# Squares of o summed in pairs of rows before the product with ones

## The chip, the cores and the metric

The kernel runs on one core of a Trainium2 chip. Its time is the device time of one execution in microseconds; three runs gave 1356.24, 1356.35 and 1356.97, a median of 1356.35. The engines are called PE (matrix products; PEld its weight loads), ACT, DVE, POOL and SP, as in the profile.

## The reference, cut to what matters

```python
kv = einsum('bhsd,bhse->bhde', k, v)            # 8 batches, 8 heads, 576 tokens, 64 wide
out = einsum('bhsd,bhde->bhse', q, kv)
rms = sqrt(mean(out * out, axis=-1) + 1e-06)    # over the 64 of one head
x = (out / rms * g_norm), heads side by side    # 4608 tokens x 512
h = x @ w_in;  g = softplus(h);  y = g @ w_out  # 512 -> 2048 -> 512
m = max(y @ w1, y @ w2, y @ w3)                 # 512 -> 768
return m @ w_out2                               # 768 -> 512
```

All is float32.

## The kernel before, in words

Tokens run along the free dimension. The 4608 tokens are done in five passes of twice 456 or 464 tokens (`NS`); in a pass every large layer is a set of products over 2x2 blocks. Pass 0 multiplies the blocks plainly and meanwhile converts the weights and stores their sums; passes 1 to 4 use seven products for eight (`run_group`, `ORDER`), with the sums of weight blocks loaded again. Each float32 operand is split into a high part that PE reads in its faster format (`F32R`) and a low part, the rest, so that one product is three instructions on PE (`mm3`, lines 155 to 157): high by high, high by low, low by high. ACT makes the high part (`cast`, L139), DVE or POOL the low part by a subtraction (`split`, L145).

Attention works on pairs of heads, so that a pair's 2 x 64 values of d fill 128 rows. For each batch `kv_mm` takes k as the stationary operand and v as the moving one and makes, for each of four pairs, two 64x64 blocks on the diagonal of a 128x128 matrix that is zero elsewhere (`heads_mm`, L513); `kv_evict` splits it into `kvh` and `kvl`. `out_mm` multiplies it with q (tokens along the free dimension): o, 128 rows (a pair's two heads, one above the other) by 456 or 464 tokens, in a bank of PSUM. The square chain then follows, 8 times a pass:

- `square`: ACT squares o into `sq` (L635), ACT casts it to `sh` (L139), DVE or POOL subtracts to `sl` (L145), ACT scales o by the gain into `og` (L638).
- `ssq_mm`: two products with `ones` (L645 with sh, L646 with sl), added in one bank, `ss`. `ones` is 1 in two 64x64 blocks on the diagonal, so that every row of ss holds the sum of squares of its head.
- `root` (L175) and `norm` (L653 to L661): reciprocal root, refined once, times og: x.

The first pass makes its o in the opening with unsplit operands (`square32`, `ssq_mm32`, `ones32`); this has no low part. For passes 1 to 4 the eight chains are made beside the products of the pass before, in its last layers but one (`attention_beside`), 32 chains in all. `at(t + 0.4, square, ...)` and `at(t + 4.8, ssq_mm, ...)` give each step its place in an order that is written in units of six PE instructions; `t` grows by 6 from chain to chain.

Events are traced in the order of these times, and a planner then orders each engine's instructions by its own estimate of when their inputs are ready. Where `pinned` is used, an engine's instructions keep the traced order from event to event: all engines in the opening, SP and ACT in the end of pass 0 (the first of the four stretches with chains), SP alone around the starts of passes and through pass 1, and elsewhere none. The chain's tiles come from one set of ten (`ctile`), and o and ss from two banks (`at`; ss of the first stretch has bank `W`).

The host lays out the inputs before the launch (`_laid_out`): `vp` is v by pairs of heads, `gn` the gain for 128 rows, `w_in` with its rows in the order of x.

Of the kernel before, what the change touches and what calls it, by code (L numbers as in the profile page):

```python
# [8 lines left out]
F32 = mybir.dt.float32  # L9
F32R = mybir.dt.float32r  # L10
I32 = mybir.dt.int32
U32 = mybir.dt.uint32
AF = mybir.ActivationFunctionType
ALU = mybir.AluOpType

B, H, S, D = 8, 8, 576, 64
NT, DM, DFF, DF2 = B * S, H * D, 2048, 768
P = 128
NS = (456, 464, 464, 464, 456)
NPASS = len(NS)  # L20
TOK = [2 * sum(NS[:i]) for i in range(NPASS + 1)]
NMAX = max(NS)
NP = H // 2
NC = 5
REST = 64
SHARED = 2
KC = DM // P
# [40 lines left out]
def kernel(  # L68
# [12 lines left out]
    nc = tc.nc  # L81
# [23 lines left out]
    def psum(tag, name):  # L105
        return ps.tile([P, 512], F32, tag=tag, bufs=PS_BUFS[tag], name=name)

    def wide(pool, tag, bufs, name, n, dtype=F32):
        return pool.tile([P, NMAX], dtype, tag=tag, bufs=bufs, name=name)[:, 0:n]

    def ctile(name, n, dtype=F32):
        return wide(cp, "c", 10, name, n, dtype)
# [7 lines left out]
    def xr_tile(p, name, n):  # L120
        return xc_tile(name, n) if p == 0 else wide(rp, "xr", 8, name, n)
# [7 lines left out]
    ones = const.tile([P, P], F32R, name="ones")  # L129
    ones32 = const.tile([P, P], F32, name="ones32")  # L130
    kvs = []
    for s in range(2):
        hi = const.tile([P, NP, P], F32R, name=f"kvh{s}")
        lo = const.tile([P, NP, P], F32R, name=f"kvl{s}")
        kvs.append((hi, lo))

    def cast(eng, hi, src):
        if eng is nc.scalar:
            nc.scalar.copy(hi, src)  # L139
        else:  # L140
            eng.tensor_copy(hi, src)

    def split(eng_hi, src, hi, lo, eng_lo):
        cast(eng_hi, hi, src)
        eng_lo.tensor_tensor(out=lo, in0=src, in1=hi.bitcast(F32), op=ALU.subtract)  # L145
# [4 lines left out]
    def sub(eng, o, a, b):  # L150
        eng.tensor_tensor(out=o, in0=a, in1=b, op=ALU.subtract)  # L151
# [315 lines left out]
    kv_t, q_t, kv_ps = {}, {}, {}  # L467
    qs, o_t, sq_t, ss_t, og_t, ra_t = {}, {}, {}, {}, {}, {}
# [29 lines left out]
    def chunks(b, p):  # L498
        def at_(parts, c):
            return next(t[:, c - cs.start] for t, cs in parts if c < cs.stop)  # L500

        whole = NC - (b < SHARED)
        for c in range(whole):
            yield [at_(parts, c) for parts in kv_t[b, p]]
        if b < SHARED:
            rows = slice(p % 2 * REST, (p % 2 + 1) * REST)
            yield [at_(parts, NC - 1)[rows] for parts in kv_t[b, p - p % 2]]

    def heads_mm(acc, b, p):
        for c, (k, v) in enumerate(chunks(b, p)):  # L510
            for j in range(2):
                r = slice(j * D, (j + 1) * D)
                nc.tensor.matmul(acc[r, r], k[:, r], v[:, r], start=(c == 0), stop=(c == NC - 1))  # L513

    def kv_mm(b):
        kv_ps[b] = psum("at", "kvps")
        for p in range(NP):
            heads_mm(kv_ps[b][:, p * P:(p + 1) * P], b, p)

    def kv_evict(b):  # L520
        hi, lo = kvs[b % 2]
        src = kv_ps.pop(b).rearrange("r (p d) -> r p d", p=NP)
        blocks = [(slice(j * D, (j + 1) * D), slice(None), slice(j * D, (j + 1) * D)) for j in range(2)]
        for b in blocks:
            cast(nc.scalar, hi[b], src[b])
        for b in blocks:
            sub(nc.vector, lo[b], src[b], hi[b].bitcast(F32))


    kv32 = {}  # L530
# [6 lines left out]
    def kv_mm32(b, p):  # L537
        acc = kv_ps[b, p] = psum("at", "kvps")[:, 0:P]
        if b + p:
            heads_mm(acc, b, p)  # L540
            return
        for c, (k, v) in enumerate(chunks(b, p)):
            nc.tensor.matmul(acc, k, v, start=(c == 0), stop=(c == NC - 1))
        warm(2)
# [9 lines left out]
    def kv_evict32(b, p, eng):  # L554
        src, dst = kv_ps.pop((b, p)), kv32[b, p]
        for j in range(2):
            r = slice(j * D, (j + 1) * D)
            cast(eng, dst[r, r], src[r, r])

    def kv_split(b):  # L560
        hi, lo = kvs[b % 2]
# [68 lines left out]

    def square(a, n, p):
        o = o_t.pop((a, p))
        sq = ctile("sq", n)
        sh, sl = ctile("sh", n, F32R), ctile("sl", n, F32R)
        nc.scalar.activation(sq, o, AF.Square)  # L635
        split(nc.scalar, sq, sh, sl, nc.vector if p % 2 or a < TOK[2] or a in TOK else nc.gpsimd)
        og = xr_tile(1, "og", n)
        nc.scalar.mul(og, o, gcol)  # L638
        sq_t[a, p] = (sh, sl)
        og_t[a, p] = og  # L640

    def ssq_mm(a, n, p, tag="at"):
        sh, sl = sq_t.pop((a, p))
        ss = psum(tag, "ss")[:, 0:n]
        nc.tensor.matmul(ss, ones, sh, start=True, stop=False)  # L645
        nc.tensor.matmul(ss, ones, sl, start=False, stop=True)  # L646
        ss_t[a, p] = ss

    def norm(a, n, p):
# [353 lines left out]

    for t in (ones, ones32, *kvs[0], *kvs[1]):
        nc.gpsimd.memset(t if t is ones32 else t.bitcast(F32), 0.0)
    for j in range(2):
        r = slice(j * D, (j + 1) * D)
        nc.gpsimd.memset(ones[r, r].bitcast(F32), 1.0)
        nc.gpsimd.memset(ones32[r, r], 1.0)
    nc.gpsimd.memset(epsc, EPS)  # L1010

    def load_gain():
# [101 lines left out]
    for n, step in enumerate(OPENING):  # L1114
        name, _, opt = step.partition(":")
        kind, *index = name.split(".")
        t = OPEN + 0.25 * n
# [61 lines left out]
def _laid_out(inputs):  # L1179
    import numpy as np  # L1180

    q, k, v = inputs["q"], inputs["k"], inputs["v"]

    def rows(a):

        a = a.reshape(B, NP, 2, S, D).transpose(0, 1, 3, 2, 4).reshape(B, NP, S, P)
        a = np.pad(a, ((0, 0), (0, 0), (0, NC * P - S), (0, 0)))
        a[:SHARED, 0::2, -REST:] = a[:SHARED, 1::2, S - REST:S]
        return np.ascontiguousarray(a.reshape(B, NP, NC, P, P).transpose(0, 1, 3, 2, 4)).reshape(B, NP, P, NC * P)

    def cols(w):

        n = w.shape[1] // P
        return np.ascontiguousarray(w.reshape(KC, P, n, P).transpose(2, 1, 0, 3)).reshape(n, P, KC * P)


    wo = inputs["moe_w_out"].reshape(4, 2, 2, P, 2, 2, P).transpose(0, 5, 4, 3, 2, 1, 6)

    w2 = inputs["moe2_w_out"].reshape(3, 2, P, 2, 2, P).transpose(3, 2, 1, 4, 0, 5)
    w2 = w2.reshape(2, P, 2, 3, 2, P).transpose(3, 0, 1, 2, 4, 5)  # L1200
    w2 = np.ascontiguousarray(w2).reshape(6, P, DM)
    return {
        "qt": np.ascontiguousarray(q.transpose(1, 3, 0, 2)).reshape(NP, P, NT),
        "kp": rows(k),
        "vp": rows(v),
        "gn": np.tile(inputs["g_norm"], 2).reshape(P, 1),
        "w_in": cols(inputs["moe_w_in"]),
        "w_out": np.ascontiguousarray(wo).reshape(NF, P, DM),
        "w123": np.ascontiguousarray(
            np.stack([cols(inputs[f"moe2_w{j}"]) for j in (1, 2, 3)], axis=1)  # L1210
        ),
        "w2_out": w2,
    }
# [25 lines left out]
```

## Time and profile before

| | |
|---|---|
| median of three runs | 1356.35 us |
| the profiled execution | 1356.71 us |
| its span, first to last instruction | 1354.9 us |
| busy, PE / PEld | 1348.7 / 1198.5 us |
| busy, DVE / ACT / POOL | 820.1 / 734.5 / 651.6 us |
| instructions, PE / DVE / ACT / POOL | 6962 / 1301 / 1426 / 613 |
| mean granted TensorE clock | 1.00 of 2.4 GHz |

Busy time is the union of an engine's instructions. Products on PE overlap in the record: one of 464 columns lasts 0.37 us there, and the next starts 0.21 us after it. A wait in square brackets is the idle time of the engine just before the instruction, and what ended it. The four stretches in which the chains run are about 204 to 290, 475 to 548, 738 to 811 and 1000 to 1072 us.

### The profile page before, as it was taken

Reading aid. Unit: us, or ns where it says so; the run is one execution under the profiler, and the core shown is the slowest. Engines: PE = TensorE matmul, PEld = TensorE weight load, DVE = VectorE, ACT = ScalarE, POOL = GpSimd, SP = SyncE. Lnnn points to the kernel's source line nnn. Section 1 sums busy time; section 2 is a strip of 40 time slices with the busy share of each in tenths; the row PEclk is TensorE's granted clock in tenths of the full one; section 3 lists DMA queues with packets and bytes.
Section 4 is the critical chain, followed back from the end, with each engine's and each line's share of the span. In section 5 each row is a group of like instructions: output and inputs, shape, how many; then the busy total and the mean of one; then the engine's idle time right before and its main releaser. Section 6 shows DMA issues by size and latency. Waiting matters only on the chain.

```text
span 1354.9 us, 20412 instructions
## 1 busy us (share of the span) xinstructions
PE 1348.7 (100%) x6962; PEld 1198.5 (88%) x6962; DVE 820.1 (61%) x1301; ACT 734.5 (54%) x1426; POOL 651.6 (48%) x613
## 2 busy tenths in 40 slices
PE   9999999999999999999999999999999999999998
PEld 6889999998888888888888888888888889998897
DVE  6856757883555767734556676445667754457444
ACT  6776657873655366446444664554356546443332
POOL 6866545665645635345335344444434444336320
PEclk9999999999999999999999999999999999999999
DMA  8799889777999686587678766766766577666765
GB/s 294 245 320 345 269 297 340 262 254 262 317 333 320 229 316 220 182 313 208 208 239 270 243 194 207 271 209 209 246 197 212 170 282 218 217 217 187 228 200 172
DMA packets 135143, 336.12 MB, mean 248 GB/s; under 512 B 14464, under 2 KB 40448, under 8 KB 135040
## 3 DMA queue, kind: packets, MB, share of 16 engines
q1 hardware_dynamic: 134576, 333.90, 74.2%
q8 instruction: 56, 0.92, 0.3%
q10 hardware_dynamic: 432, 0.92, 0.2%
q14 instruction: 47, 0.39, 0.1%
q0 software_dynamic: 32, 0.00, 0.0%
HBM read 269.35 MB, written 65.40 MB: 247 GB/s over the span
## 4 chain that ended last, share of the span: by engine, by line
PE 97%; ACT 1%; DMA 1%; POOL 0%; DVE 0%; issue 0%; SPq 0%; POOLq 0%; ACTq 0%
PE Xo L155 6%; PE Xo L156 6%; PE Xo L157 6%; PE Xx L157 5%; PE Xx L155 5%; PE Xx L156 5%; PE Xh L155 5%; PE Xh L157 5%; PE Xh L156 5%; PE Yo L155 3%; PE Yo L156 3%; PE Yo L157 3%; PE Yx L155 3%; PE Yx L156 3%; PE Yx L157 3%; PE Yh L155 3%
## 5 line engine op out<-in xcount | busy, mean ns | idle before, releaser
L145 POOL TENSOR_TENSOR lo<-e,hi 128x464 fp32r<-128x464 f32 (+1 forms) x160 | 188.5, 1214 | 176.7 <-ACT hi L139 162.9
L139 ACT CAST hi<-t 128x464 fp32r<-128x464 f32 (+1 forms) x120 | 65.7, 547 | 124.7 <-DVE e L151 55.1
L155 PE MATMUL Xo<-hi,u 128*128 128x464 f32 (+1 forms) x296 | 110.7, 375 | 0.1
L156 PE MATMUL Xo<-lo,u 128*128 128x464 f32 (+1 forms) x296 | 109.9, 371 | 0.0
L157 PE MATMUL Xo<-hi,u 128*128 128x464 f32 (+1 forms) x296 | 109.9, 371 | 0.0
L148 DVE TENSOR_TENSOR x<-x,Xx 128x464 f32<-128x464 f32 (+1 forms) x104 | 65.5, 632 | 56.8 <-PE Xx L157 56.5
L155 PE MATMUL Xh<-hi,u 128*128 128x464 f32 (+1 forms) x266 | 99.3, 373 | 0.4 <-DVE lo L151 0.2
L157 PE MATMUL Xh<-hi,u 128*128 128x464 f32 (+1 forms) x266 | 98.9, 372 | 0.2 <-POOL u L151 0.2
L156 PE MATMUL Xh<-lo,u 128*128 128x464 f32 (+1 forms) x266 | 98.6, 371 | 0.0
L139 ACT CAST hi<-e 128x464 fp32r<-128x464 f32 (+1 forms) x160 | 86.0, 581 | 20.3 <-PE Yx L156 16.9
L139 ACT COPY m<-Xo 128x464 f32<-128x464 f32 (+1 forms) x108 | 58.6, 548 | 69.3 <-PE Xo L157 67.2
L145 DVE TENSOR_TENSOR lo<-t,hi 128x464 fp32r<-128x464 f32 (+1 forms) x120 | 75.8, 636 | 33.5 <-ACT hi L139 31.2
L155 PE MATMUL Xx<-hi,u 128*128 128x464 f32 (+1 forms) x256 | 95.1, 371 | 0.0
L157 PE MATMUL Xx<-hi,u 128*128 128x464 f32 (+1 forms) x256 | 95.0, 371 | 0.0
L156 PE MATMUL Xx<-lo,u 128*128 128x464 f32 (+1 forms) x256 | 94.8, 370 | 0.0
L151 POOL TENSOR_TENSOR e<-e 128x464 f32<-128x464 f32 (+1 forms) x32 | 38.2, 1192 | 106.2 <-DVE t L151 83.2
L145 POOL TENSOR_TENSOR lo<-m,hi 128x464 fp32r<-128x464 f32 (+1 forms) x40 | 47.8, 1212 | 74.3 <-ACT hi L139 74.3
L145 POOL TENSOR_TENSOR u<-sw,u 128x256 fp32r<-128x256 f32 (+1 forms) x67 | 67.7, 1024 | 32.9 <-ACT u L139 32.4
L139 ACT CAST u<-sw 128x512 fp32r<-128x512 f32 (+1 forms) x120 | 62.7, 540 | 33.2 <-POOL sw L151 16.5
L151 POOL TENSOR_TENSOR sw<-sw 128x256 f32<-128x256 f32 x84 | 66.6, 796 | 23.2 <-DVE sw L280 19.1
L148 DVE TENSOR_TENSOR Wh<-h,Wh 128x464 f32<-128x464 f32 (+1 forms) x32 | 20.6, 644 | 92.3 <-PE Wh L157 74.2
L661 POOL TENSOR_TENSOR og<-og,r 128x464 f32<-128x464 f32 (+1 forms) x32 | 40.4, 1262 | 68.2 <-DVE r L657 42.5
(261 smaller groups left out, 4104.8 us busy)
## 6 DMA issues: line engine op xcount, KB each, us to landing
u<-wd SPq DMA_DIRECT2D x241, 512.0 KB, 4.5
ux<-wd SPq DMA_DIRECT2D x99, 512.0 KB, 3.6
wd<-u SPq DMA_DIRECT2D x161, 256.0 KB, 4.9
u<-wd SPq DMA_DIRECT2D x104, 256.0 KB, 4.1
raw<-in_w_out_dram SPq DMA_DIRECT2D x22, 512.0 KB, 4.6
raw<-in_w_dram SPq DMA_DIRECT2D x18, 512.0 KB, 4.6
raw<-in_w_in_dram SPq DMA_DIRECT2D x16, 512.0 KB, 5.6
wd<-ahead SPq DMA_DIRECT2D x32, 256.0 KB, 6.3
```

The lines of the kernel that those rows point to most:

```text
L139: nc.scalar.copy(hi, src)
L145: eng_lo.tensor_tensor(out=lo, in0=src, in1=hi.bitcast(F32), op=ALU.subtract)
L148: eng.tensor_tensor(out=o, in0=a, in1=b, op=ALU.add)
L151: eng.tensor_tensor(out=o, in0=a, in1=b, op=ALU.subtract)
L155: nc.tensor.matmul(acc, wh, xh, start=first, stop=False, skip_group_check=on)
L156: nc.tensor.matmul(acc, wh, xl, start=False, stop=False, skip_group_check=on)
L157: nc.tensor.matmul(acc, wl, xh, start=False, stop=last, skip_group_check=on)
L661: nc.gpsimd.tensor_tensor(out=og, in0=og, in1=r, op=ALU.mult)
```

## The change

The rows of o are put into another order: rows 0 to 63 hold the first 32 values of d of both heads, rows 64 to 127 the last 32 of both. Row r and row r + 64 then belong to the same head. To this end the columns of v, the gain and the rows of w_in are reordered on the host (`mixed`), and `head(t, j)` picks head j's columns, two runs of 32, wherever the kernel wrote 64 neighbouring ones: the outputs and moving operands of `heads_mm`, the evictions of kv, and the ones.

`square` now squares the upper and the lower half of o apart, each into 64 rows starting at row 0 (`sq`, `half`), and adds them; the sum's high part goes to rows 0 to 63 of one tile `hl` and its low part to rows 64 to 127. The add runs on POOL where the subtraction runs on DVE, and the other way round. `ssq_mm` is one product with ones. Row r of ones is 1 in the columns of head (r // 32) % 2. The opening's chain (`square32`) is not changed beyond the order of rows.

```diff
--- before.py
+++ after.py
@@ -506,11 +506,14 @@
             rows = slice(p % 2 * REST, (p % 2 + 1) * REST)
             yield [at_(parts, NC - 1)[rows] for parts in kv_t[b, p - p % 2]]
 
+    def head(t, j):
+        return t.rearrange("r (i j d) -> r i j d", i=2, j=2)[:, :, j]
+
     def heads_mm(acc, b, p):
         for c, (k, v) in enumerate(chunks(b, p)):
             for j in range(2):
                 r = slice(j * D, (j + 1) * D)
-                nc.tensor.matmul(acc[r, r], k[:, r], v[:, r], start=(c == 0), stop=(c == NC - 1))
+                nc.tensor.matmul(head(acc[r], j), k[:, r], head(v, j), start=(c == 0), stop=(c == NC - 1))
 
     def kv_mm(b):
         kv_ps[b] = psum("at", "kvps")
@@ -519,12 +522,17 @@
 
     def kv_evict(b):
         hi, lo = kvs[b % 2]
-        src = kv_ps.pop(b).rearrange("r (p d) -> r p d", p=NP)
-        blocks = [(slice(j * D, (j + 1) * D), slice(None), slice(j * D, (j + 1) * D)) for j in range(2)]
-        for b in blocks:
-            cast(nc.scalar, hi[b], src[b])
-        for b in blocks:
-            sub(nc.vector, lo[b], src[b], hi[b].bitcast(F32))
+        src = kv_ps.pop(b)
+
+        def block(t, j):
+            t = t[j * D:(j + 1) * D]
+            return t.rearrange("r (p i j d) -> r (p i) j d", p=NP, i=2, j=2)[:, :, j]
+
+        hi, lo = (t.rearrange("r p d -> r (p d)") for t in (hi, lo))
+        for j in range(2):
+            cast(nc.scalar, block(hi, j), block(src, j))
+        for j in range(2):
+            sub(nc.vector, block(lo, j), block(src, j), block(hi, j).bitcast(F32))
 
 
     kv32 = {}
@@ -555,7 +563,7 @@
         src, dst = kv_ps.pop((b, p)), kv32[b, p]
         for j in range(2):
             r = slice(j * D, (j + 1) * D)
-            cast(eng, dst[r, r], src[r, r])
+            cast(eng, head(dst[r], j), head(src[r], j))
 
     def kv_split(b):
         hi, lo = kvs[b % 2]
@@ -630,20 +638,23 @@
 
     def square(a, n, p):
         o = o_t.pop((a, p))
-        sq = ctile("sq", n)
-        sh, sl = ctile("sh", n, F32R), ctile("sl", n, F32R)
-        nc.scalar.activation(sq, o, AF.Square)
-        split(nc.scalar, sq, sh, sl, nc.vector if p % 2 or a < TOK[2] or a in TOK else nc.gpsimd)
+        sq, half = (ctile(name, n)[0:D] for name in ("sq", "half"))
+        hl = ctile("hl", n, F32R)
+        engines = [nc.gpsimd, nc.vector]
+        if not (p % 2 or a < TOK[2] or a in TOK):
+            engines.reverse()
+        for t, rows in ((sq, o[0:D]), (half, o[D:P])):
+            nc.scalar.activation(t, rows, AF.Square)
+        add(engines[0], sq, sq, half)
+        split(nc.scalar, sq, hl[0:D], hl[D:P], engines[1])
         og = xr_tile(1, "og", n)
         nc.scalar.mul(og, o, gcol)
-        sq_t[a, p] = (sh, sl)
+        sq_t[a, p] = hl
         og_t[a, p] = og
 
     def ssq_mm(a, n, p, tag="at"):
-        sh, sl = sq_t.pop((a, p))
         ss = psum(tag, "ss")[:, 0:n]
-        nc.tensor.matmul(ss, ones, sh, start=True, stop=False)
-        nc.tensor.matmul(ss, ones, sl, start=False, stop=True)
+        nc.tensor.matmul(ss, ones, sq_t.pop((a, p)), start=True, stop=True)
         ss_t[a, p] = ss
 
     def norm(a, n, p):
@@ -1003,10 +1014,10 @@
 
     for t in (ones, ones32, *kvs[0], *kvs[1]):
         nc.gpsimd.memset(t if t is ones32 else t.bitcast(F32), 0.0)
-    for j in range(2):
-        r = slice(j * D, (j + 1) * D)
-        nc.gpsimd.memset(ones[r, r].bitcast(F32), 1.0)
-        nc.gpsimd.memset(ones32[r, r], 1.0)
+    for i in range(4):
+        r = slice(32 * i, 32 * i + 32)
+        nc.gpsimd.memset(head(ones[r], i % 2).bitcast(F32), 1.0)
+        nc.gpsimd.memset(head(ones32[r], i % 2), 1.0)
     nc.gpsimd.memset(epsc, EPS)
 
     def load_gain():
@@ -1181,17 +1192,19 @@
 
     q, k, v = inputs["q"], inputs["k"], inputs["v"]
 
-    def rows(a):
-
-        a = a.reshape(B, NP, 2, S, D).transpose(0, 1, 3, 2, 4).reshape(B, NP, S, P)
+    mixed = np.arange(P).reshape(2, 2, 32).transpose(1, 0, 2).reshape(P)
+
+    def rows(a, order=slice(None)):
+
+        a = a.reshape(B, NP, 2, S, D).transpose(0, 1, 3, 2, 4).reshape(B, NP, S, P)[..., order]
         a = np.pad(a, ((0, 0), (0, 0), (0, NC * P - S), (0, 0)))
         a[:SHARED, 0::2, -REST:] = a[:SHARED, 1::2, S - REST:S]
         return np.ascontiguousarray(a.reshape(B, NP, NC, P, P).transpose(0, 1, 3, 2, 4)).reshape(B, NP, P, NC * P)
 
-    def cols(w):
+    def cols(w, order=slice(None)):
 
         n = w.shape[1] // P
-        return np.ascontiguousarray(w.reshape(KC, P, n, P).transpose(2, 1, 0, 3)).reshape(n, P, KC * P)
+        return np.ascontiguousarray(w.reshape(KC, P, n, P)[:, order].transpose(2, 1, 0, 3)).reshape(n, P, KC * P)
 
 
     wo = inputs["moe_w_out"].reshape(4, 2, 2, P, 2, 2, P).transpose(0, 5, 4, 3, 2, 1, 6)
@@ -1202,9 +1215,9 @@
     return {
         "qt": np.ascontiguousarray(q.transpose(1, 3, 0, 2)).reshape(NP, P, NT),
         "kp": rows(k),
-        "vp": rows(v),
-        "gn": np.tile(inputs["g_norm"], 2).reshape(P, 1),
-        "w_in": cols(inputs["moe_w_in"]),
+        "vp": rows(v, mixed),
+        "gn": np.tile(inputs["g_norm"], 2)[mixed].reshape(P, 1),
+        "w_in": cols(inputs["moe_w_in"], mixed),
         "w_out": np.ascontiguousarray(wo).reshape(NF, P, DM),
         "w123": np.ascontiguousarray(
             np.stack([cols(inputs[f"moe2_w{j}"]) for j in (1, 2, 3)], axis=1)
```

## Rows read from the trace of the kernel before

**Rows 1.** The page: span and instructions; chain that ended last, by engine.

```profile
span 1354.9 us, 20412 instructions
...
PE 97%; ACT 1%; DMA 1%; POOL 0%; DVE 0%; issue 0%; SPq 0%; POOLq 0%; ACTq 0%
```

**Rows 2.** Waits of PE's weight loads, 48:1355: total us, times, longest (3 of 18).

```profile
PEld Xo L155 <- ACT m L139: 2.8, 11, 0.4
...
PEld ss L646 <- DVE sl L145: 0.4, 1, 0.4
...
PEld Xo L156 <- DVE lo L145: 0.2, 1, 0.2
```

**Rows 3.** Four stretches: us, then busy us and count of PE, PEld, DVE, ACT, POOL.

```profile
204.00:290.00 86.00, 86.00 (x503) 78.28 (x502) 72.90 (x108) 68.39 (x134) 52.62 (x57) 1.00 0.87 295
475.00:548.00 73.00, 72.98 (x413) 64.06 (x412) 48.26 (x76) 47.31 (x91) 31.93 (x26) 1.00 0.77 268
738.00:811.00 73.00, 73.00 (x434) 65.37 (x433) 48.72 (x76) 46.03 (x88) 28.61 (x24) 1.00 0.70 232
1000.00:1072.00 72.00, 71.89 (x352) 64.50 (x351) 48.83 (x76) 46.54 (x89) 28.76 (x25) 1.00 0.67 211
```

**Rows 4.** Timeline of PE: start us, us; products with ones, and the next.

```profile
213.58 0.37 PE L645 MATMUL ss<-sh,ones 128*128 128x464 f32 x1
213.79 0.37 PE L646 MATMUL ss<-sl,ones 128*128 128x464 f32 x1
214.00 0.37 PE L155 MATMUL Xo<-hi,u 128*128 128x456 f32 x1
```

**Rows 5.** Instructions of tile sq: duration ns min/median/max, first and last start.

```profile
L635 ACT ACTIVATE sq<-o x32: 532/558/587, 206.3 to 1062.6; 128x464 f32<-128x464 f32 x24, 128x456 f32<-128x456 f32 x8
...
L145 DVE TENSOR_TENSOR sl<-sq,sh x26: 620/642/1657, 207.9 to 1064.7; 128x464 fp32r<-128x464 f32 x20, 128x456 fp32r<-128x456 f32 x6
...
L145 POOL TENSOR_TENSOR sl<-sq,sh x6: 1176/1195/1203, 517.0 to 1055.5; 128x464 fp32r<-128x464 f32 x4, 128x456 fp32r<-128x456 f32 x2
```

**Rows 6.** Timeline of ACT: a cast on 64 partitions.

```profile
734.62 0.37 ACT L139 CAST kvh<-kvps 64x256 fp32r<-64x256 f32 x1 [0.23 <-PE kvps L513]
```

**Rows 7.** Groups by shape, count, busy us, mean ns: half as many elements a partition.

```profile
L139 ACT CAST u<-sw 128x256 fp32r<-128x256 f32 x45 | 17.6, 406 | 6.6 <-DMA wd<-u 5.7 <-POOL sw L151 0.7
...
L151 POOL TENSOR_TENSOR sw<-sw 128x256 f32<-128x256 f32 x84 | 66.6, 796 | 23.2 <-DVE sw L280 19.1
```

**Rows 8.** Timeline of ACT: one chain's square, og and cast.

```profile
476.25 0.56 ACT L635 ACTIVATE sq<-o 128x464 f32<-128x464 f32 x1
476.70 0.66 ACT L638 ACTIVATE og<-o,gcol 128x464 f32<-128x464 f32 x1
...
478.56 0.58 ACT L139 CAST sh<-sq 128x464 fp32r<-128x464 f32 x1
```

**Rows 9.** Timelines around three chains: subtraction, and product that reads it.

```profile
207.91 0.64 DVE L145 TENSOR_TENSOR sl<-sq,sh 128x464 fp32r<-128x464 f32 x1 [1.03 <-ACT sh L139]
...
492.71 0.19 PEld L646 LDWEIGHTS ss<-sl,ones 128*128 128x128 f32 x1 [0.38 <-DVE sl L145]
...
804.83 3.91 POOL L145 TENSOR_TENSOR lo<-m,hi 128x464 fp32r<-128x464 f32 x3
...
806.03 1.66 DVE L145 TENSOR_TENSOR sl<-sq,sh 128x464 fp32r<-128x464 f32 x1 [1.72 <-ACT sh L139]
...
807.88 0.37 PE L646 MATMUL ss<-sl,ones 128*128 128x464 f32 x1
```

**Rows 10.** Timeline of PE: one block of k-v products.

```profile
732.02 2.55 PE L513 MATMUL kvps<-v,k 128*64 128x64 f32 x80
```

**Rows 11.** Timelines of POOL and DVE at the start: a memset, the gain's columns.

```profile
2.87 0.14 POOL L1008 MEMSET ones<- 64x64 f32 x1
...
9.43 0.15 DVE L1017 TENSOR_SCALAR gcol<-gcol 128x1 f32<-128x1 f32 x1
11.57 0.69 DVE L612 SCALAR_TENSOR_TENSOR og<-o,gcol,r 128x456 f32<-128x456 f32 x1 [1.99 <-ACT r L175]
```

## The prediction

> **What bounds the kernel now.** I read the page first. The chain of waits that ended last is 97% PE over a span of 1354.9 us [rows 1]: the time is that of the queue of matrix products, and any other engine matters only where a product waits for it. So the second view is who the weight loads of PE waited for, from 48 us on, when the opening is over [rows 2]. Its 18 rows sum to 10.5 us. The reader is to see two of them: eleven waits for ACT's copy of a product's bank (2.8 us in all, 0.4 at most) and a single wait of 0.4 us for the square chain that is changed here. The third view cuts out the four stretches in which o is made for the next pass, with eight square chains each [rows 3]. PE is busy throughout at a granted clock of 1.00. The others have room, though unequally: in the first stretch DVE is at 72.9 of 86 us, ACT at 68.4, POOL at 52.6; in the other three DVE and ACT are near two thirds and POOL near two fifths. A product of these shapes therefore costs the kernel its distance to the next product's start, if nothing new makes PE wait.
>
> **What is removed.** Each of the 32 chains has two products with ones, of sh and of sl; one is left. The two start 0.21 us apart, and so does what follows [rows 4] (a busy time of 0.37 us overlaps its successor's, and is not the price). 32 x 0.21 = 6.7 us off PE's queue. One load of ones goes with each and is hidden today under the product before.
>
> By the Trainium skill (TensorE: Matmul & The Clock Gate, section Back-to-back issue gap) a lone product's distance is its columns over 2.4 GHz plus 2.5 ns, an estimate of 0.196 us for 464 columns; 32 of them would be 6.3 us, and the forecast 0.4 us higher. The trace says 0.21, so the trace's value stands.
>
> **What is added.** The chain was: ACT squares o into sq, ACT casts sh, DVE (26 times) or POOL (6 times) subtracts to sl; these take 0.56, 0.58, and 0.64 or 1.19 us [rows 5]. Now ACT squares twice, 64 rows each; the two halves are added (POOL where DVE subtracts afterwards, 26 times; DVE in the other six); then the same cast and subtraction on 64 rows. No row has these operations on 64 rows, so I bound them. ACT casts 64x256 in 0.37 us [rows 6] against 0.41 for 128x256 [rows 7]: halving the partitions saves next to nothing, so a half square, cast or subtraction costs at least nine tenths of its row, and I take all of it. For the add on POOL, time that goes with all elements would be that of 128x256, 0.80 us [rows 7]; time that goes with elements a partition is 1.19 [rows 5]. I take 1.19, since ACT's rows speak for the second.
>
> In busy time that is ACT + 32 x 0.56 = 17.9 us, POOL + 26 x 1.19 = 30.9, DVE + 6 x 0.63 = 3.8. In the first stretch it makes ACT 68.4 + 4.5 = 72.9 of 86 us and POOL 52.6 + 9.5 = 62.1; in the third, with six POOL adds and two on DVE, ACT 50.5 of 73, POOL 35.7, DVE 50.0 [rows 3]. No engine passes PE, so this costs nothing by itself; what hides it is the stream of products, about 40 of them between one chain and the next. Without that cover it would be the 17.9 us of ACT.
>
> **What is longer.** What may cost is when the chain is done. ACT starts two neighbouring operations 0.45 us apart (476.25 and 476.70 [rows 8]), so the second square adds 0.45 and the add 0.80 to 1.19, 1.25 to 1.65 us in all; 1.1 where DVE adds. In the trace the subtraction ends before the second product starts in 31 of 32 chains, by 5.2 us at most (208.55 to 213.79, [rows 4, 9]), by 0.2 at least (807.69 to 807.88), and with a median near 2.2; the last of the 32 is the 0.4 us wait at 492.71 [rows 9]. Nine of the 32 have less than what is added. If every product with ones kept its place among the others, their shortfalls (read off chain by chain, 1.65 or 1.1 less the margin) would sum to 6.9 us, and as the remaining product needs both halves at the place of the first one, 0.2 us earlier, 8.7: the whole gain and more. But the order isn't kept: the planner places each instruction by when it believes its inputs ready. [Rows 8] shows it: og, written after the cast of sh, ran before it, and sh started 1.75 us after the square had ended. A longer chain moves the product with ones behind other products, which are independent of it and always at hand; what PE pays is only where the planner's times are off.
>
> The added wait: the cast on ACT now waits for the add. Queued behind it in ACT's order are the copies of product banks for which PE waits most often already [rows 2]. On POOL the add queues behind runs of up to three subtractions, 3.91 us at 804.83 [rows 9]. The multiplication that makes og needs only o, and can run meanwhile, so o's bank comes free little later. What is late next is r from the ss bank, which feeds og's scaling; x is combined from it only after the last group of the pass, and I cost that at nothing. If that cover is gone, x of the next pass is late by the same 1.65 us, once a pass.
>
> New waits of PE: the lower bound is -3.2 us (the waits for ACT's copies and for sl [rows 2] all vanish in the reshuffle), the upper 8.7. I take +1.2: five more waits of 0.25 us, the mean of the eleven, about one chain in six. That is near the low end, because the trace with its 32 chains so placed has one such wait.
>
> **What is moved.** The columns of v, gain and w_in are reordered before the launch, which costs no time on the chip. The k-v products write two runs of 32 columns instead of one of 64 and read v likewise. Six blocks of 80 take 2.55 us each [rows 10]. No row shows a product with such runs. Below zero there is no reason for a gain, as the columns are the same; above, each run costs as much as a whole product now and the blocks double, 6 x 2.55 = 15.3 us. I take 0, by the nearest row, as columns and products are the same in number. ACT and DVE read and write 64x256 in such runs when they evict; six evictions that doubled would add 6 x 2 x 0.37 = 4.4 us to ACT, beside PE's work: 0. At the start POOL has four memsets more, 0.14 us each [rows 11], perhaps 0.5 us, ahead of the load of the gain, whose scaled column was ready at 9.58 and used at 11.57 [rows 11]: hidden by 2.0 us; with that gone it would be 0.5 us. No DMA is added or moved past another by the edit itself; loads that wait for PE's progress go up to 1.7 us a pass earlier.
>
> **Sum.** The profiled execution took 1356.7 us (span 1354.9 and 1.8 around it). 1356.7 - 6.7 + 1.2 = 1351.2; it lies 0.4 above the median of the runs, so 1350.8 there.
>
> **Rivals.**
> *The waits eat the gain.* The planner leaves the products with ones about where they are and the longer chain stalls PE in the nine tight places: 1356.35 - 6.7 + 6.9 = 1356.6, no change. For it: margins of 0.2 to 1.6 us where the planner thought just enough; POOL runs of 3.9 us before an add. Against it: one wait in 32 today.
> *DVE held by POOL's adds* (the slower side). At 806.03 a subtraction on DVE with both inputs in SBUF took 1.66 us instead of 0.64 while POOL ran three of its own [rows 9]. The place is the 26 adds on POOL, the price up to 1.02 us of DVE each, and its results are what PE reads next. At half of it, PE waits 26 x 0.5 = 13 us: 1350.8 + 13 = 1363.8. It decides against the kernel from (2.7 + 5.5) / 26 = 0.32 us an add. Against it: POOL is already busy for 142 us in these stretches [rows 3], and PE's list of waits hardly shows DVE there.
> The Trainium skill states the lock behind it (SBUF — State Buffer, section Who interferes with whom): a DVE instruction with two SBUF inputs and a GpSimd one that reads SBUF exclude each other for the whole instruction, whichever starts first. The 1.66 us agrees. By that rule each add can hold DVE once for its full length, 26 x 1.19 = 31 us of DVE at most, in stretches where DVE has some 85 us free.
> *The split runs cost PE.* The blocks of k-v products double: 1350.8 + 15.3 = 1366.1. It decides against the kernel once they are 54% longer. For it: no row shows such a pattern. Against it: nothing in the number of columns changes.
> That the change doesn't do what it says could only mean that a second product stays; the code issues one.
>
> **Numbers.** 0.80 for the forecast, whose own range is 1348.0 to 1353.3 (1348.0: no new waits and half of the present 3.2 us gone; 1353.3: 3.7 us of new waits in place of 1.2); 0.11 for the eaten gain, 0.05 for DVE held, 0.03 for the split runs, 0.01 for none of these. The range for all reaches from 1348.0 to 1356.0: some 0.03 lies below it, and above it half of the eaten gain and the two slow cases. A measurement tells 0.2%, 2.7 us, from no change. Faster, under 1353.6: nearly all of the forecast, 0.79. Same: the eaten gain and the forecast's tail, 0.13. Slower: 0.08.
>
> **What would show it.** In the profile after: 32 products with ones of hl instead of 64, and still 0.21 us to the next; about 32 products fewer in PE's row and the span 5 to 6 us shorter, all of it between 204 and 1072 us, 1.3 to 1.5 us in each stretch; half squares of 0.5 to 0.56 us; POOL adds near 1.2 (0.8 would mean that partitions count). PE's waits for hl, and for ACT's copies, summing to under 3 us more than now. A block of k-v products still at 2.55 us. I am wrong if PE's list of waits shows more than 3 us for hl or for ACT in the stretches, if DVE's subtractions there stretch beyond 1 us as a rule with PE behind them, or if the k-v blocks grow.

## The result, and the profile after

The changed kernel takes 1373.42 us (median of four, 1372.73 to 1373.90) against 1356.30 before: the ratio is 1.012, with a 95% interval of 1.0107 to 1.0132. 17 us slower, where 5.5 us faster was forecast. Of the page, the head and the chain that ended last:

```profile
span 1370.9 us, 20388 instructions
...
PE 1350.5 (99%) x6930; PEld 1190.8 (87%) x6930; DVE 824.8 (60%) x1307; ACT 756.4 (55%) x1458; POOL 683.9 (50%) x643
...
PE 83%; ACT 4%; DMA 4%; DVE 4%; POOL 3%; issue 2%; SPq 1%; POOLq 0%; ACTq 0%; DVEq 0%
```

PE has its 32 products fewer, and the chain that ended last, 97% PE before [rows 1], is 83% PE: followed back from its end, it now leads through others' work too. PE itself was idle for 20.4 us of its span (1370.9 less 1350.5), where it had been for 6.2. Whom its weight loads waited for, from 48 us on (us in all, times, longest), answers to [rows 2]:

```profile
PEld ss L657 <- DVE hl L145: 8.8, 8, 3.5
PEld Xo L155 <- ACT m L139: 4.6, 15, 0.5
PEld ss L657 <- POOL hl L145: 3.5, 6, 1.7
PEld Yo L155 <- DVE m L148: 2.6, 3, 1.3
PEld Xo L157 <- DVE u L145: 1.9, 3, 1.4
```

All 25 rows sum to 35.1 us, against 10.5 before. The two rows of `ss` are the new product waiting for its operand: 12.3 us, against 0.4. Of the other three only the copies of Xo were there, with 2.8 us. The four stretches, in the columns of [rows 3] (then granted clock, DMA share, GB/s):

```profile
204.00:290.00 86.00, 82.15 (x475) 72.54 (x474) 67.19 (x99) 68.27 (x132) 58.14 (x60) 1.00 0.82 272
475.00:548.00 73.00, 71.02 (x393) 59.81 (x392) 50.24 (x78) 48.55 (x93) 38.34 (x31) 1.00 0.71 250
738.00:811.00 73.00, 71.90 (x485) 62.01 (x485) 48.87 (x76) 47.68 (x92) 36.66 (x30) 1.00 0.70 231
1000.00:1072.00 72.00, 70.09 (x403) 60.81 (x403) 49.35 (x79) 47.39 (x91) 36.87 (x30) 1.00 0.61 200
```

PE was idle there for 0.1 us at most before; now it is for 1 to 4 us in each (the worst stall, shown next, lies just behind the third window, as the chains run later). ACT, DVE and POOL are about as full as forecast, or less: POOL at 58.1 us in the first stretch and 36.7 in the third, forecast 62.1 and 35.7. Taken by the start of the next pass's first product (324.3, 584.3, 847.3, 1106.8 before; 330.7, 592.7, 861.2, 1122.7 after), the four stretches lose 6.4, 2.0, 5.5 and 2.0 us: all of the 16 us of the span.

The worst stall shows how such a wait comes about. It is the last chain of the third stretch; timelines of PE, POOL, ACT and DVE (start us, us; in brackets the idle time before and its releaser):

```profile
816.71 0.37 PE L157 MATMUL Yo<-hi,u 128*128 128x464 f32 x1
820.25 0.75 PE L657 MATMUL ss<-hl,ones 128*128 128x464 f32 x1 [3.16 <-DVE hl L145]
820.80 0.59 PE L155 MATMUL Xo<-hi,u 128*128 128x464 f32 x1
821.18 0.59 PE L156 MATMUL Xo<-lo,u 128*128 128x464 f32 x1
```

```profile
815.13 2.35 POOL L145 TENSOR_TENSOR lo<-m,hi 128x464 fp32r<-128x464 f32 x2
817.42 1.15 POOL L148 TENSOR_TENSOR sq<-sq,half 64x464 f32<-64x464 f32 x1
```

```profile
818.60 0.58 ACT L139 CAST hl<-sq 64x464 fp32r<-64x464 f32 x1 [1.56 <-POOL sq L148]
819.09 0.53 ACT L883 COPY m<-Xo 128x464 f32<-128x464 f32 x1
```

```profile
819.21 0.98 DVE L145 TENSOR_TENSOR hl<-sq,hl 64x464 fp32r<-64x464 f32 x1 [4.62 <-ACT hl L139]
820.12 0.63 DVE L148 TENSOR_TENSOR Wo<-m,Wo 128x464 f32<-128x464 f32 x1
```

Both halves were squared by 815.9. The add stood behind two subtractions on POOL until 817.42; ACT, at the cast, stood idle for it, with the copy of a product's bank next in its queue; DVE stood idle for the cast; PE for DVE. None of the three took up a later instruction meanwhile: ACT stood still for 1.56 us, DVE for 4.62, PE for 3.16. So one late add holds three queues, and what stands behind is late too.

Over all 32 chains, the idle time of engines ahead of the instructions of `hl`, and who waited for it (us, times):

```profile
  ACT hl L139: 32.1, 20
  POOL sq L148: 19.1, 22
...
  DVE hl L145: 30.6, 19
  PEld ss L657: 12.3, 14
```

The subtraction's engine sat idle for the cast (first row) and ACT for the add (second): 51 us of idle queues. Before, ACT never waited ahead of this cast, and the subtraction's engine 11.0 us for it.

### The profile page after: what moved, and what is told of

The parts are those of the page before. It is cut to its first block, busy times and chain, and to the rows that moved or that the text cites. A ratio compares the mean times of both kernels' runs of the same rounds, so it can differ in the third digit from the quotient of the medians.

```text
span 1370.9 us, 20388 instructions
## 1 busy us (share of the span) xinstructions
PE 1350.5 (99%) x6930; PEld 1190.8 (87%) x6930; DVE 824.8 (60%) x1307; ACT 756.4 (55%) x1458; POOL 683.9 (50%) x643
## 4 chain that ended last, share of the span: by engine, by line
PE 83%; ACT 4%; DMA 4%; DVE 4%; POOL 3%; issue 2%; SPq 1%; POOLq 0%; ACTq 0%; DVEq 0%
PE Xx L155 5%; PE Xx L157 5%; PE Xx L156 5%; PE Xh L155 5%; PE Xh L157 5%; PE Xh L156 5%; PE Xo L155 4%; PE Xo L157 3%; PE Xo L156 3%; PE Yx L155 3%; PE Yx L156 3%; PE Yx L157 3%; PE Yh L155 3%; PE Yh L157 3%; PE Yh L156 3%; DMA wd<-u 2%
## 5 line engine op out<-in xcount | busy, mean ns | idle before, releaser
L139 ACT CAST hi<-e 128x464 fp32r<-128x464 f32 (+1 forms) x160 | 86.0, 580 | 20.3 <-PE Yx L156 17.2
L151 POOL TENSOR_TENSOR sw<-sw 128x256 f32<-128x256 f32 x84 | 66.6, 794 | 23.3 <-DVE sw L280 18.7
L175 ACT ACTIVATE e<-h 128x464 f32<-128x464 f32 (+1 forms) x64 | 37.9, 592 | 58.9 <-DVE h L148 58.9
```

The costliest lines, as they stand in the source:

```text
L175: tables["used"].append(nc.scalar.activation(out, src, func, **kw).ins)
```

## The experiments

Each ran beside the kernel before, whose median lay between 1356.9 and 1357.5 (1356.3 for the changed kernel itself). The diffs show only the lines that matter; experiments 9, 10 and 14 also have the edit of 5. In the table *change* is the kernel's median less that of the kernel before in the same comparison; *waits* is the sum of all rows of whom PE's weight loads waited for, from 48 us on, *ss* the part at the product with ones (or its first load). The ratios stand with each experiment.

| kernel | change, us | waits, us | ss, us |
|---|---|---|---|
| before | | 10.5 | 0.4 |
| 1 rows rearranged only | +0.1 | 11.8 | 0.4 |
| 5 one product fewer only | -5.8 | 11.4 | 0 |
| 9 as 5, extra square on ACT, unread | -3.7 | 14.2 | 0 |
| 14 as 5, extra work on POOL, unread | +0.3 | 18.7 | 0 |
| 6 change without the add | -0.9 | 20.0 | 4.1 |
| 7 change, add on DVE, unread | +6.3 | 24.7 | 10.9 |
| 3 change, add on DVE | +6.8 | 27.0 | 8.7 |
| 2 change, add as placed, unread | +12.4 | 31.0 | 11.7 |
| after | +17.1 | 35.1 | 12.3 |
| 16 as 3, product 0.8 units later | +10.5 | 30.4 | 1.6 |
| 15 change, product 0.8 later | +18.3 | 33.4 | 1.5 |
| 8 change, cast and product later | +18.5 | 33.5 | 4.0 |
| 4 change, product 1.7 later | +21.6 | 40.4 | 2.2 |
| 13 before, product 1.7 later | +6.2 | 17.4 | 0.4 |
| 11 before, product 2.4 earlier | +17.7 | 30.2 | 17.2 |
| 12 high part only, no cast, no subtraction | -6.9 | 11.1 | 0 |

In every row the change in time is within 4 us of the change in waits, less 6.7 us where a product is gone. So PE's waits account for the time of these kernels. The profile of 6 is of its slowest run (1359.03, median 1356.04), so its waits are high for its time. Experiment 10 is not in the table: nearly all of its loss lies in and just behind the opening.

**1. The rows alone.** The rearrangement stays, the chain is that of before.

```diff
-        add(engines[0], sq, sq, half)
...
+        split(nc.scalar, sq, sh, sl, nc.vector if p % 2 or a < TOK[2] or a in TOK else nc.gpsimd)
```

> The rearranged rows alone (v, gain, w_in, kv blocks in two runs of 32), with the square chain of before: one square of 128 rows, sh, sl, two products with ones. Theory W (the longer chain holds up queues that are worked in order: the cast on ACT waits for the add, the subtraction on DVE for the cast, the product on PE for the subtraction) and theory L (31 us more of POOL and 18 us more of ACT, and POOL's adds holding DVE): 1356.3 us, between 1354.5 and 1358. Theory R (the runs of 32, or the planner's reshuffle that they set off, cost the time): 1370 or more.

1357.57 against 1357.51, ratio 1.000 (0.9991 to 1.001). Runs of 32 columns, the host's order and the memsets cost nothing: the loss is in the chain.

**2. The add, unread.** The same instructions, but the cast and the subtraction don't wait for the sum.

```diff
-        add(engines[0], sq, sq, half)
+        add(engines[0], half, sq, half)
```

> All of the change, but the add writes its sum where nothing reads it, and the cast and the subtraction read the first half's squares at once: the sum of the second half is left out, the work on every engine is the same. W: the chain is as short as before the change, so the 6.7 us of the removed products show: 1349 to 1353 us. L: the load is unchanged, so 1368 to 1374. R: 1368 to 1374.

1369.91, 1.0088 (1.0073 to 1.0103). The wait for the add in its place is worth under 5 us. But the run replaces one price by another: freed of the order, subtractions on DVE now run beside work on POOL. Timelines of DVE and POOL:

```profile
1073.37 5.25 DVE L145 TENSOR_TENSOR hl<-sq,hl 64x456 fp32r<-64x456 f32 x1
```

```profile
1072.17 1.44 POOL L148 TENSOR_TENSOR half<-sq,half 64x456 f32<-64x456 f32 x1 [1.76 <-ACT half L647]
1073.57 1.16 POOL L672 TENSOR_TENSOR og<-og,r 128x456 f32<-128x456 f32 x1
1074.70 3.42 POOL L145 TENSOR_TENSOR lo<-m,hi 128x464 fp32r<-128x464 f32 x3
```

A subtraction of 0.64 us took 5.25 and ended 0.5 us after POOL's run of four. What DVE's TENSOR_TENSOR operations of two SBUF inputs took beyond 0.64 us each (DVE's excess from here on), summed over 200 to 300, 470 to 560, 730 to 830 and 995 to 1100 us, is 42.0 us here, against 19.9 before and 19.7 after.

**3. All adds on DVE.**

```diff
-        add(engines[0], sq, sq, half)
+        add(nc.vector, sq, sq, half)
```

> All of the change, with all 32 adds on DVE (0.63 us) instead of 26 on POOL (1.2 us). W: the chain is 0.55 us shorter and no longer waits behind POOL's runs of subtractions, so about half of the loss goes: 1358 to 1364 us. L in the form of POOL's adds holding DVE: the loss goes, 1350 to 1354; L in the form of mere load on DVE: 1372 or more, as DVE has 17 us more. R: 1368 to 1374.

1364.34, 1.0047 (1.003 to 1.0064): 10.3 us of the 17 are due to POOL having the add. 6.8 remain, with DVE at 74.9 of 86 us in the first stretch and 51.6 to 55.4 of 72 or 73 in the others.

**4. Product, root and scaling later in the order written** (4.8 to 6.5 units, the rest likewise).

```diff
-            at(t + 4.8, ssq_mm, a, n, p, "W" if pas == 1 else "at")
+            at(t + 6.5, ssq_mm, a, n, p, "W" if pas == 1 else "at")
```

> All of the change, and the product with ones, the root and the norm come 1.7 units (about ten products) later in the written order. W: the direct waits of PE for hl, 12.3 us in the trace, go, while ACT and DVE are still held up by the cast and the subtraction: 1357 to 1363 us. L and R: no change, 1370 to 1375.

1379.07, 1.0154 (1.0139 to 1.0169): slower still, which I did not expect. The waits at ss are nearly gone, and others stand in their place:

```profile
PEld Xo L155 <- ACT m L139: 10.9, 23, 1.5
PEld o L156 <- DVE ql L145: 5.4, 5, 1.8
```

**5. One product fewer, nothing else**: the kernel before without the low part's product; its subtraction still runs.

```diff
-        nc.tensor.matmul(ss, ones, sl, start=False, stop=True)
+        low_t.append(sl)
```

> The kernel before, in which only the second of the two products with ones is left out (the low part sl is still made, and nothing reads it): the removal by itself. All theories: 32 x 0.21 = 6.7 us less than before, 1348 to 1351 us, if PE's queue sets the time as the profile says. If it is under 4 us, the removed products were not worth their distance.

1351.16, 0.9958 (0.9943 to 0.9973). The removal is worth 5.8 us, by the interval 3.7 to 7.7. The product that is left reads only the high part, so this kernel doesn't wait for the subtraction any more; in the trace of before PE's wait for it was 0.4 us.

**6. The change without the add.** Both squares are made, one is not summed.

```diff
-        add(engines[0], sq, sq, half)
```

> All of the change without the add (the second half's squares are made and not summed; the cast reads the first half's at once). W: no engine waits for POOL in the middle of the chain, 1349 to 1354 us. L, if POOL's load and lock are the cause: the same. L, if the 18 us more of ACT are the cause: 1365 or more. Against the run whose add was done but unread (1369.9) it tells what the add costs as work beside the subtraction on DVE.

1356.04, 0.9994 (0.9985 to 1.0004), where 1349 to 1354 was expected. That is 4.9 us more than experiment 5, and two things are new: a second square, 0.56 us of ACT, before the cast, and a product that again needs the low part, now at the place of the first of the two products. By that place alone the trace of before gives 1.4 us of shortfall. The chain, from the first square to the end of the subtraction, is 3.2 us on the mean against 3.0. No run tells the two apart.

**7. The add on DVE, unread.**

```diff
-        add(engines[0], sq, sq, half)
+        add(nc.vector, half, sq, half)
```

> All of the change, the 32 adds on DVE, with sums that nothing reads. Beside the run with the adds on DVE and read (1364.3): same work on every engine, no wait of the cast for the add. W: 1352 to 1358 us. L (the work on DVE): 1363 to 1366.

1363.18, 1.0052 (1.0032 to 1.0072), the same as experiment 3. With the add on DVE its being read makes no difference that the runs can tell. That in 26 of the chains the subtraction stands behind the add in the same queue either way may be the reason; it was not traced.

**8. Cast and subtraction as a step of their own at t + 3**, the product as in experiment 4.

```diff
+            at(t + 3, split_sum, a, n, p)
```

> All of the change; the cast and the subtraction are a step of their own 2.6 units later in the written order, and the product with ones, root and norm 1.7 units later. W: other work of ACT and DVE goes ahead of the cast and the subtraction instead of standing behind them, so ACT's and DVE's waits in the chain (22 and 31 us in the trace of the change) fall below 10 each and the time is 1351 to 1358 us. L: the work is the same, 1370 to 1380.

1375.43, 1.0136 (1.0121 to 1.0151). Against the change nothing was won; against experiment 4, which has the product in the same place, some 3 us. ACT no longer idles for the add (0 us), and the subtraction's engine for the cast only 12.5 us (7.2 on DVE, 5.2 on POOL). But the idle time moved forward: the add's engine now idles 47.1 us for the second square, against 14.1 in the change. So the run doesn't show what idle engines cost by themselves.

**9. ACT's load alone**: experiment 5 with an unread square of half the rows.

```diff
+        nc.scalar.activation(og[0:D], o[D:P], AF.Square)
         nc.scalar.mul(og, o, gcol)
```

> The kernel with one product left out (1351.2 us: the chain of before, the low part's product omitted), and on ACT one more square of 64 rows a chain, 0.56 us, which nothing waits for (it is written where og overwrites it). Theory Q (any work added to an engine's queue in these stretches makes what stands behind it later, and PE waits for that): 1354 to 1357 us, as much as the second square cost in the change without its add (1356.0). Theory M (only what lies between o and the product with ones counts, since PE waits for hl): 1351 to 1352.

1353.43, 0.9974 (0.9964 to 0.9984). 17.9 us more on ACT, with no one waiting for the result, cost about 2 of the 5.8 us. The rest of experiment 6's 4.9 is left to what only that run has: the second square ahead of the cast, and a product that needs the low part.

**10. POOL's load alone, a first attempt**: experiment 5 with three subtractions of constants a chain.

```diff
+                sub(nc.gpsimd, ones32[0:D], ones32[0:D], ones32[0:D])
```

> The same base of 1351.2 us, and on POOL in 26 of the chains three subtractions on 64x128 of a constant that nothing reads, together about as long as one add (1.2 us). Q: POOL's own subtractions come later and DVE is held by the lock, 1354 to 1360 us. M: 1351 to 1352.

1380.00, 1.0172 (1.0156 to 1.0187), and inconclusive: having no late input, all 78 ran at 31 to 84 us. The first product into Xx starts at 87.9 us, where it was 61.0 in experiment 5, so nearly all of the loss stands before the chains. They say nothing on the chains.

**14. The same with operands that pin it to its chain** (og, read by nobody after).

```diff
+                sub(nc.gpsimd, ones32[0:D], og[0:D, 0:P], og[0:D, 0:P])
```

> The kernel with one product left out (1351.2 us), and on POOL in 26 of the chains three subtractions on 64x128 that read og, so that they can't run before it, and whose result nothing reads; together 1.2 us, as one add. Theory Q (load and lock): 1354 to 1360 us. Theory M (only the chain's length against the place of its product): 1351 to 1353.

1357.41, 0.9999 (0.9989 to 1.0009). Group by shape, then one of the places, DVE:

```profile
L151 POOL TENSOR_TENSOR ones<-og x78: 388/398/872, 207.0 to 1064.8; 64x128 f32<-64x128 f32 x78
```

```profile
231.07 1.32 DVE L145 TENSOR_TENSOR sl<-sq,sh 128x464 fp32r<-128x464 f32 x1
```

About 31 us of POOL work in 78 pieces, for which no one waits, cost 6.0 us over experiment 5. DVE's excess, summed as in experiment 2, rises to 32.6 us, from 18.9 in experiment 5.

**11. The kernel before with less margin**: the products with ones 2.4 units earlier, no work added.

```diff
-            at(t + 4.8, ssq_mm, a, n, p, "W" if pas == 1 else "at")
+            at(t + 2.4, ssq_mm, a, n, p, "W" if pas == 1 else "at")
```

> The kernel before, with its two products with ones, and root and norm, 2.4 units (some 14 products) earlier in the written order, so that their place is no longer behind the chain's end by the written order but where the planner believes their inputs ready. No work is added. M: PE now waits for sl in many chains, 1359 to 1365 us. Q: no change, 1355.5 to 1358.

1374.80, 1.0133 (1.0116 to 1.0149): by an earlier place of the products, root and norm, without an instruction more, the loss of the change, and more than either theory expected. PE's waits at ss are 17.2 us of it.

```profile
PEld ss L646 <- POOL sl L145: 6.8, 6, 1.5
PEld ss L646 <- DVE sl L145: 6.3, 14, 1.1
...
PEld ss L645 <- ACT sh L139: 4.1, 3, 2.7
```

**13. The kernel before with more margin**: 6.5 for 4.8, as in experiment 4.

> The kernel before, with its products with ones, root and norm 1.7 units later in the written order (as in the run of the change that took 1379.1). If the move itself is bad (the product then stands behind the next chain's o in the order, and root and norm beside its squares): 1361 us or more. If it is bad only for the longer chain: 1356 to 1358.

1363.36, 1.0048 (1.0033 to 1.0063). So the later place costs 6.2 us by itself, with hardly a wait at ss to be saved. In experiment 4 the same move saved 10 us of waits at ss and still cost the changed kernel some 4.5 us.

**15 and 16. A small step later** (4.8 to 5.6), for the change and for experiment 3.

```diff
-            at(t + 4.8, ssq_mm, a, n, p, "W" if pas == 1 else "at")
+            at(t + 5.6, ssq_mm, a, n, p, "W" if pas == 1 else "at")
```

> All of the change, with the product with ones, root and norm 0.8 units (some five products, 1 us) later, still ahead of the next chain's o. M: part of the margin is back: PE's wait for hl falls from 12.3 to under 6 us, 1362 to 1369 us. If later places are bad in themselves: 1373 to 1378.

> The change with all adds on DVE (1364.3 us), with the product with ones, root and norm 0.8 units later. M: the wait for hl (8.7 us in that trace) falls to under 3, 1356 to 1361 us. If later places are bad in themselves: 1364 to 1370.

1375.42, 1.014 (1.0122 to 1.0159), and 1367.69, 1.0078 (1.0063 to 1.0093): no better. In 15 the waits at ss fall from 12.3 to 1.5 us, and these grow (followed back as in the next section, 19.8 of the other 31.9 us lead to the chain's cast, add or subtraction):

```profile
PEld Xo L155 <- ACT m L139: 13.2, 19, 4.6
PEld Yo L155 <- DVE m L887: 4.3, 5, 1.2
```

**12. Remove work instead**: ACT writes the square straight into PE's faster format; no cast, no subtraction, one product. The low bits of the squares are left out.

```diff
-        sq = ctile("sq", n)
+        sq = ctile("sq", n, F32R)
-        split(nc.scalar, sq, sh, sl, nc.vector if p % 2 or a < TOK[2] or a in TOK else nc.gpsimd)
```

> The kernel before without the low part of the squares: ACT writes the squares in the faster format at once, there is no cast, no subtraction and one product with ones (the squares' low bits are left out). Both theories: the removed product without any added work, and 18.6 us of ACT and 17 us of DVE less: 1348 to 1351 us, less than both kernels.

1350.25, 0.995 (0.9935 to 0.9965), faster than both kernels.

```profile
span 1348.5 us, 20260 instructions
...
PE 1341.6 (99%) x6930; PEld 1191.9 (88%) x6930; DVE 802.4 (60%) x1275; ACT 719.6 (53%) x1394; POOL 641.2 (48%) x607
```

PE has as many products as in the changed kernel. That is some 1 us better than experiment 5, which the intervals don't tell apart: ACT's and DVE's relief is worth little here.

## Why the prediction was wrong

**The step that failed** is "New waits of PE": +1.2 us, at most 8.7. It measured +24.6 (35.1 less 10.5), and the prediction's own sign of being wrong, over 3 us of waits for hl, came out at 12.3. Two sentences led there. The first: "A longer chain moves the product with ones behind other products, which are independent of it and always at hand". It did not move. Counted in PE's order from the last product of a chain's o to the first product with ones, 29 of the 32 chains have as many products between them as before (24 in most); the other three have 5, 7 and 12 more. The evidence that I gave, og running before the cast, was of ACT's order and not of PE's.

The chain did grow by about what I had added, 1.25 to 1.65 us: from the start of the first square to the end of the subtraction it took 3.0 us on the mean before (2.2 to 4.3, once 7.5) and 4.6 after (3.6 to 5.9, once 8.8). So the added time came out of the margin. From the subtraction's end to the product that reads its result it was 2.2 us at the median and is 0.3; in 12 of the 32 chains it is 0.05, which is no margin. In single chains the growth is up to 2.8 us (2.7 in the stall above, where the add waited 1.5 us for POOL). That one wait in 32 stood in the trace of before showed that the place fitted the chain of then. It was no evidence for a chain with one engine more.

Second, the upper bound of 8.7 counted only the product with ones, and the sum behind it does not come out of the trace. By its own 1.65 and 1.1 us, seven chains and not nine fall short, by 4.9 us together and not 6.9; at the first product's own start, which in one chain is 1.5 us earlier than the second's and not 0.2, ten fall short, by 9.9 and not 8.7. Its waits are 12.3 us. Nearly 13 us more arose at products for which nothing was changed: 22.8 us stand there, against 10.1 before. I followed each of these waits back, for up to 7 us, through what ended it and what stood before that in its engine's queue. 8.8 of the 22.8 us lead to the chain's second square, add, cast or subtraction; of the 10.1 before, none lead to the chain. One of them, on DVE and PEld: an add of 1.10 us, the operation behind it, and PE's wait for that.

```profile
787.63 1.10 DVE L148 TENSOR_TENSOR sq<-sq,half 64x464 f32<-64x464 f32 x1
788.66 0.62 DVE L148 TENSOR_TENSOR m<-m,Yo 128x464 f32<-128x464 f32 x1
```

```profile
789.34 0.19 PEld L155 LDWEIGHTS Yo<-hi,ux 128*128 128x128 f32 x1 [1.25 <-DVE m L148]
```

I had named ACT's queue ("queued behind it in ACT's order are the copies") and priced it at nothing.

**"No engine passes PE, so this costs nothing by itself"** failed too, by a smaller sum. Off the chain, ACT's second square costs about 2 us (experiment 9) and POOL's work 6.0 (experiment 14), with all engines below PE.

The loss, step by step, by the changes in time of experiments 5, 6, 3 and after: product gone -5.8; second square, and a product that needs the low part, +4.9; an add, on DVE, +7.7; the add on POOL instead, +10.3; together +17.1. Each step carries an uncertainty of some 2 us.

**The terms one by one.** Product gone: -6.7 forecast, -5.8 measured, and the distance to the next is 0.21 us as before:

```profile
256.07 0.38 PE L657 MATMUL ss<-hl,ones 128*128 128x464 f32 x1
256.28 0.32 PE L155 MATMUL o<-qh,kvh 128*128 128x352 f32 x1
```

Half squares and POOL's adds lasted what was taken for them, so the partitions hardly count (DVE's six adds took 0.72 us at the median, taken as 0.63); min, median, max in ns:

```profile
L647 ACT ACTIVATE half<-o x32: 548/555/559, 207.0 to 1078.7; 64x464 f32<-64x464 f32 x24, 64x456 f32<-64x456 f32 x8
L148 POOL TENSOR_TENSOR sq<-sq,half x26: 1148/1183/1619, 207.7 to 1079.3; 64x464 f32<-64x464 f32 x20, 64x456 f32<-64x456 f32 x6
```

The split runs are free; a block of k-v products is as in [rows 10]:

```profile
740.38 2.55 PE L516 MATMUL kvps<-v,k 128*64 128x64 f32 x80
```

The memsets are hidden (gain's column ready at 9.95, used at 10.76). So nearly every duration was right and the sum was wrong: what it missed is waits.

**The rivals.** *The waits eat the gain* had the mechanism: the products with ones stayed where they were. Its price was little over a quarter of what came: 6.9 us of shortfalls where 24.6 of waits arose, 12.3 of them at these products. *The split runs* are refuted by experiment 1. *DVE held by POOL's adds* is not what the changed kernel shows: DVE's excess is 19.7 us, as before. There DVE mostly idles for the cast while the add runs. Take that order away (experiment 2) or only add load (14), and DVE is held instead. POOL's work costs some 6 us then (2 against 7, and 14 against 5), and 10.3 where the cast waits for the add (after against 3). The Trainium skill (SBUF — State Buffer, section Who interferes with whom) has a GpSimd instruction that reads SBUF and a DVE one of two SBUF inputs shut each other out for a whole instruction. The trace agrees, and adds that one DVE instruction can sit out several of POOL's on end: 5.25 us in experiment 2. My reading in the prediction, once and for one length, was too mild.

**Open.** Why the planner left the products in their place, and where its estimates part from the chip, was not traced; nor where the 3.9 us come from by which PE's other waits grew without leading back to the chain; an order with the product placed by hand from measured times was not tried. The 6.2 us that the later place costs even in the kernel before (13) stand in PE's waits for copies (+3.2) and for q's low part (`ql`, +3.4); why these come late was not traced.

## What to carry to other kernels

On a kernel whose bottleneck engine never idles, the other engines' busy share is not slack: price an added operation by what stands behind it in each in-order queue of its chain, and bound it by all waits of the bottleneck, not only by those for the changed operand. A margin read from the old trace belongs to the old chain: take the product's place among the others as fixed until the bottleneck's own order shows that it moves, and set the chain's growth against the margin. Before trading bottleneck time for work elsewhere, time the removal alone, the load alone without readers, and the two chained: here -5.8, +2 to +6, and +17.

## What the chip showed beyond that

In the stall shown above, the granted clock fell; columns as for the stretches:

```profile
816.00:820.00 4.00, 1.09 (x6) 0.62 (x4) 0.79 (x1) 2.42 (x5) 3.69 (x4) 1.00 0.65 231
820.20:823.40 3.20, 3.15 (x8) 2.76 (x9) 1.73 (x3) 2.34 (x3) 0.00 (x0) 0.50 0.01 3
824.00:828.00 4.00, 4.00 (x21) 3.57 (x20) 2.54 (x5) 1.52 (x4) 2.11 (x2) 1.00 0.01 2
```

After PE's 3.16 us of idle time it is 0.50 from 820.2 to 823.4 us, the 1.2 GHz level, and products start 0.385 us apart instead of 0.21; from 48 to 800 and from 830 to 1369 us it is 1.00. The nine starts from 820.25 on take 3.50 us to 823.75, where 9 x 0.21 = 1.9 would do: 1.6 us on top, half as much again as the wait. And two neighbouring half squares start 0.56 to 0.58 us apart in 31 of the 32 chains (206.46 and 207.02 in the first), not the 0.45 that I read from a square and the scaling that followed it: there the second square costs ACT its full duration.
